# A gated mix of two spectral filters on one core: one product instruction a unit, the negations on VectorE, half of the gate later, and a new order list

## The chip, the cores and the metric

The kernel runs on one core of a Trainium2 chip. The metric is the device time of one execution in microseconds (us); three executions took 115.3, 115.53 and 116.19, median 115.53. TensorE (PE) multiplies matrices into PSUM, VectorE (DVE), ScalarE (ACT) and GpSimd (POOL) do elementwise work, and SyncE (SP) issues nearly all transfers. Each engine works through its own instructions in order.

## The reference

Both branches filter the same `x` (2048 rows by 1024 columns, bf16) in the frequency domain, with weights A and B. A gate per row mixes the two results.

```python
def _ref(x, w_r, w_i):                       # A and B alike
    B, S, D = x.shape
    X = jnp.fft.rfft2(x.astype(jnp.float32), axes=(-2, -1))
    X = X * (w_r + 1j * w_i)
    return jnp.fft.irfft2(X, s=(S, D), axes=(-2, -1)).astype(jnp.bfloat16)

g = sigmoid((x * gate_w).sum(-1, keepdims=True))
return g * _ref(x, A_w_r, A_w_i) + (1 - g) * _ref(x, B_w_r, B_w_i)
```

## The kernel before

The transforms are matrix products with constant matrices. The 2048 rows are taken as 128 x 16 (`s1` from 0 to 15 is a slab of 128 rows), the columns are folded into sums and differences ("even" and "odd" frequencies), and the frequency rows are worked in 16 units: units 0 to 7 are even, 8 to 15 odd. A unit covers two groups of 64 frequency rows, 256 columns each.

The program is written down as a list, `ORDER`. Its tokens are executed from left to right, each calls one small function, and every engine's instructions come in the order of their tokens. So the list alone decides what stands behind what on each engine and in SP's queue of transfers; the tile pools and the semaphores add the waits. A token's last letter often names the engine (A for ScalarE, D for VectorE, P for GpSimd, S for SP), and the last digit of a TensorE token is its PSUM bank (of eight; some take two banks, from that digit on).

The tokens, by stage:

- **Load.** `x:S:s:n` loads n slabs, `c:S:..` constants, `W:S:n` the weights of unit n (512 KB). W 0 to 7 go into the tile `ro`, 8 to 11 into `wx`, 12 to 15 into the tile `y` (once the even half of `y` has been used up). `tab:A` runs a small sigmoid so that ScalarE's function table is loaded.
- **First transform.** `F1:s:e/o` multiplies a slab's half (eight matmuls, L331). Then either `FC` copies one part out of PSUM and `FD` (VectorE, two instructions) folds it into `y`, or `FX` copies both parts and `FP` (GpSimd, two instructions) folds. The copies go to eight rotating pieces of `wx`.
- **Gate.** `GH`, `GC`, `GT` (four times), `GK` compute and turn the gate's transform; `GZ:h` spreads eight slabs of it over the rows (TensorE), `GS:h` takes the sigmoid of these (ScalarE, 1024 columns) into the tile `EA`. `GA:D:b` multiplies four slabs of `EA` by the constant `E`, and `GB:D:b` makes `EB` as `E` less that. `EA` and `EB` are the matrices of the second inverse transform, in which the mixing is done; slabs 8 to 15 are needed by its tokens with v of 4 and above.
- **Unit n.** `F2:n:tt` (four matmuls) and its copy `T`; `F3:n` (twelve matmuls, of which four use `WN`, the negative of the constant `WF`, made by `neg`) and its copy `X`; `P:n:r`, the products of `X` with the weights of both filters (VectorE, L505); for units 0 to 7 a correction of one column, `Y` (TensorE), `NA` and `N` (VectorE); `J:n` (32 matmuls in four groups, L548), into two pairs of banks; two copies `R:n:0` and `R:n:1` into a tile `rl`; two stores `H:n:0` and `H:n:1` (256 KB each) to scratch memory in DRAM.
- **Inverse over rows and columns.** `L:p:v` loads 512 KB of scratch back (p is 0 for the even half, into `re`, 1 for the odd half, into `ro`; v from 0 to 7). `V:p:v:s` (eight matmuls, L576) and its copy `VC`; then `C` (four matmuls of 256 columns, L601) or `U` (four of 512, L592).
- **Output.** For the even half `EX` copies out of PSUM and `EQ` mixes (VectorE or GpSimd, L626), or `ES` and `EF`, or `E`. For the odd half `OR` adds straight from PSUM (VectorE, L646), or `OC` and `OP`, or `QD` and `QP`, use GpSimd. `S:v` stores 512 KB of output, `S:v:s` half of that.

The pools have two buffers each for `T`, `X` and `V`, three for the products `p`, and five for `rl`, which the output tiles share. An `rl` buffer is free when its two stores have landed. On every copy token `cp` (L199 to L203) picks the instruction, so copies of ScalarE have line L201 and those of VectorE L203.

Products may be asked for in halves or at once:

```python
def prod(n, r):                              # L493 to L505
    ...
    if r == "b":
        xb = X[:].rearrange("p r t (a m) -> p r t a m", a=1).to_broadcast([P, 2, 2, 4, 256])
        wb = w.rearrange("p (r t) a m -> p r t a m", r=1).to_broadcast([P, 2, 2, 4, 256])
        nc.vector.tensor_tensor(p[:], xb, wb, ALU.mult)
        return
    xb = X[:, int(r)].rearrange("p t (a m) -> p t a m", a=1).to_broadcast([P, 2, 4, 256])
    nc.vector.tensor_tensor(p[:, int(r)], xb, w, ALU.mult)
```

In the list before, each unit has two tokens, `P:n:0` and `P:n:1`, and on TensorE the order within `J:n` is: first real by real, second imaginary by imaginary (which needs the other half), then the two mixed ones.

The functions that the change calls differently:

Of the kernel before, what the change touches and what calls it, by code (L numbers as in the profile page):

```python
# [10 lines left out]
P = 128  # L11
S = 2048
D = 1024
# [8 lines left out]


ORDER = """
warm:8 c:A:F1 x:S:0:1 x:S:1:1 c:A:gws x:S:2:2 tab:A F1:0:e:4 x:S:4:2 FC:0:e:D F1:1:e:7 F1:0:o:5 x:S:6:2 FC:1:e:A FD:0:e
FX:0:o:A F1:1:o:0 FD:1:e F1:2:e:6 x:S:8:2 FC:2:e:D FX:1:o:A F1:3:e:2 FD:2:e FC:3:e:A FD:3:e FP:1:o FP:0:o x:S:10:2 x:S:12:2
F1:2:o:4 F1:3:o:7 F1:4:e:0 F1:5:e:6 x:S:14:2 FX:2:o:A FP:2:o FC:4:e:D c:S:w0 c:S:WF:0:4 c:S:PM c:S:WF:4:16 c:S:EZ c:S:FD:0:1
W:S:0 W:S:1 c:S:E c:S:WJ:0:4 c:S:WJ:4:16 F1:7:e:1 FC:5:e:A W:S:2 FX:3:o:A FD:4:e FD:5:e FP:3:o F1:6:e:3 FC:7:e:A F1:5:o:4
F1:9:e:0 F1:8:e:6 F1:7:o:5 FC:6:e:A FX:5:o:A FC:9:e:A FD:7:e FD:6:e FC:8:e:A F1:11:e:1 gc:P F1:10:e:7 FX:7:o:A F1:4:o:4
F1:12:e:3 F1:13:e:2 FC:11:e:A FC:10:e:A FP:5:o FD:9:e FD:8:e FD:11:e FX:4:o:A F1:9:o:1 F1:15:e:6 F1:14:e:0 F1:11:o:5 FP:7:o  # L30
FC:12:e:A FC:13:e:A neg:A:0:4 FC:15:e:A FD:10:e FP:4:o FD:12:e FC:9:o:A F1:13:o:7 FC:14:e:A FD:13:e F1:12:o:4 F1:6:o:2
FD:15:e FD:14:e FD:9:o F2:1:0:6 FC:11:o:A neg:A:4:16 FC:13:o:A FX:6:o:A F2:1:1:3 T:1:0:A FD:13:o FC:12:o:A F1:15:o:2 T:1:1:A
FC:15:o:A FD:11:o F1:14:o:1 F1:10:o:0 F3:1:6 F2:0:0:3 F1:8:o:5 FD:12:o FC:10:o:A F2:0:1:4 FC:14:o:A FD:15:o FD:10:o F2:2:0:2
FD:14:o X:1:A FC:8:o:A T:0:0:A pw:P T:0:1:A T:2:0:A FD:8:o F2:3:0:0 F2:2:1:7 T:2:1:A F3:0:5 X:0:A P:1:1 P:1:0 P:0:1 F2:3:1:4
Y:1:3 F2:4:0:7 T:3:1:A FP:6:o F3:2:1 NA:1:D Y:0:5 W:S:9 NA:0:D W:S:3 W:S:7 P:0:0 W:S:8 W:S:11 N:1:D W:S:6 W:S:4 c:S:FD:1:2
W:S:5 c:S:IG T:4:0:A GH:6 X:2:A T:3:0:A GC:A Y:2:4 NA:2:D F2:5:1:1 P:2:0 P:2:1 W:S:10 F3:3:2 T:5:1:A F2:4:1:4 N:0:D GT:2:5
J:1:6:0 GT:0:5 X:3:A GT:1:5 GT:3:5 T:4:1:A F3:4:3 R:1:0:A F2:5:0:2 R:1:1:D X:4:A T:5:0:A GK:D J:0:6:0 F2:6:0:4 P:3:1 F2:6:1:5
Y:3:3 R:0:0:A F3:5:6 R:0:1:A P:3:0 NA:3:D GZ:0:2 F2:7:0:0 X:5:A F2:7:1:1 W:S:14 T:6:1:D T:6:0:D N:3:D N:2:D GS:0 P:4:0
T:7:0:D J:3:4:6 W:S:12 W:S:13 W:S:15 T:7:1:A GZ:1:0 R:3:1:A R:3:0:D J:2:6:2 Y:5:4 P:4:1 GS:1 Y:4:5 NA:5:D NA:4:D P:5:0 P:5:1
R:2:0:A N:4:D F3:7:0 R:2:1:A X:7:A F2:8:1:5 F3:6:6 F2:8:0:4 T:8:0:A T:8:1:D J:4:2:0 F3:8:4 H:0:0 H:1:0 X:6:A R:4:1:A Y:7:7  # L40
P:7:1 F2:9:0:6 N:5:D R:4:0:A Y:6:0 P:7:0 H:1:1 X:8:A NA:6:D T:9:0:A H:0:1 NA:7:D GA:D:4 F2:10:1:1 H:2:0 H:3:0 H:3:1 F2:9:1:0
P:6:0 T:9:1:A N:7:D P:6:1 T:10:1:A J:5:2:4 J:7:0:6 R:5:1:A R:5:0:A F2:10:0:5 H:4:0 F3:9:2 F2:11:0:4 P:8:1 H:2:1 R:7:0:A N:6:D
R:7:1:D J:6:0:6 GB:D:4 H:4:1 T:10:0:A X:9:A H:7:0 H:5:0 P:8:0 T:11:0:D R:6:0:A GA:D:0 R:6:1:A F2:11:1:2 F3:10:3 P:9:0 H:5:1
P:9:1 H:7:1 H:6:1 X:10:A H:6:0 J:8:0:6 T:11:1:A R:8:0:D R:8:1:A F2:12:0:4 H:8:0 T:12:0:A P:10:1 P:10:0 F3:11:2 F2:12:1:5
H:8:1 L:0:0 F2:14:1:1 X:11:A T:12:1:A L:0:1 GB:D:0 F2:14:0:0 F3:12:6 J:9:2:4 T:14:0:A P:11:0 T:14:1:A X:12:A R:9:1:A P:11:1
# [12 lines left out]
VC:1:1:1:A EQ:6:0:1:P EQ:7:0:0:P C:1:3:1:1 QD:3:1:1 V:1:0:0:0 EF:5:0 QD:3:0:0 U:1:1:0:6 U:1:1:1:2 QD:3:1:0 OR:1:1:0 OR:1:1:1
EQ:7:1:1:P EQ:7:0:1:P VC:1:0:1:A EQ:6:0:0:P VC:1:0:0:A OC:1:0:A V:1:2:0:4 QP:3:1:0:P OP:1:0:0 VC:1:2:0:A V:1:2:1:5 V:1:5:0:7
U:1:0:1:6 VC:1:2:1:D OR:0:1:1 U:1:2:0:2 OR:2:0:0 OR:0:1:0 OR:2:0:1 U:1:0:0:0 V:1:5:1:5 QP:3:1:1:P OC:0:0:A VC:1:5:1:A  # L60
QP:3:0:1:P OP:1:0:1 QP:3:0:0:P VC:1:5:0:D S:S:1 U:1:2:1:3 OR:2:1:0 OP:0:0:1 V:1:4:0:0 V:1:4:1:5 OR:2:1:1 S:S:3 VC:1:4:1:D
OP:0:0:0 VC:1:4:0:A U:1:5:0:6 U:1:5:1:4 U:1:4:0:7 V:1:7:1:5 U:1:4:1:1 OC:4:0:A OR:5:0:0 OR:5:1:0 S:S:2 V:1:6:1:7 VC:1:7:1:A
EQ:6:1:0:P OR:5:0:1 OR:5:1:1 OR:4:1:1 OR:4:1:0 U:1:7:1:3 S:S:0 S:S:5 OP:4:0:1 VC:1:6:1:A V:1:6:0:2 OP:4:0:0 VC:1:6:0:A S:S:4
U:1:6:1:6 V:1:7:0:4 U:1:6:0:0 VC:1:7:0:A OR:7:1:1 OR:7:1:0 OR:6:1:0 U:1:7:0:4 OR:6:1:1 OR:6:0:1 OR:6:0:0 OR:7:0:1 OR:7:0:0
S:S:7:1 S:S:6 S:S:7:0
"""


# [655 lines left out]
```

## Time and profile before

| | |
|---|---|
| median of three executions | 115.53 us |
| profiled execution: its own time | 116.1 us |
| its span, first to last instruction | 114.3 us |
| busy: TensorE, VectorE, ScalarE, GpSimd | 103.0, 100.9, 86.4, 39.5 us |
| moved by DMA | 36.79 MB, mean 322 GB/s |
| granted TensorE clock | 0.991 |

The span lies inside the execution's own time; 1.8 us are around it. A line of groups reads: source line, engine, operation, output and input tiles, shape, how many; then busy us, mean ns of one; then the idle time before them and what ended it. A line of a timeline or of the chain begins with start and duration in us. TensorE's matmuls overlap, so a busy TensorE is not one at its peak.

### The profile page before, as it was taken

Reading aid. Unit: us, or ns where it says so; the run is one execution under the profiler, and the core shown is the slowest. Engines: PE = TensorE matmul, PEld = TensorE weight load, DVE = VectorE, ACT = ScalarE, POOL = GpSimd, SP = SyncE. Lnnn points to the kernel's source line nnn. Section 1 sums busy time; section 2 is a strip of 40 time slices with the busy share of each in tenths; the row PEclk is TensorE's granted clock in tenths of the full one; section 3 lists DMA queues with packets and bytes.
Section 4 is the critical chain, followed back from the end, with each engine's and each line's share of the span. In section 5 each row is a group of like instructions: output and inputs, shape, how many; then the busy total and the mean of one; then the engine's idle time right before and its main releaser. Section 6 shows DMA issues by size and latency. Waiting matters only on the chain.

```text
span 114.3 us, 3946 instructions
## 1 busy us (share of the span) xinstructions
PE 103.0 (90%) x1616; PEld 70.3 (61%) x1619; DVE 100.9 (88%) x175; ACT 86.4 (76%) x140; POOL 39.5 (35%) x61
## 2 busy tenths in 40 slices
PE   5969999999999988989898989998999999999930
PEld 2569999875546543534453547845998966566510
DVE  0068999999998999999999999999999598998990
ACT  4054989999799899999999999999689762325400
POOL 1019999800000000000000000830382999997300
PEclk9999999999999999999999999999999999999996
DMA  3999999999999899997969999996999998099655
GB/s 75 330 331 406 405 374 318 350 338 376 398 406 416 257 361 281 376 377 245 339 232 262 393 391 301 369 386 228 335 281 351 377 390 345 3 377 398 271 222 199
DMA packets 17794, 36.79 MB, mean 322 GB/s; under 512 B 1904, under 2 KB 10736, under 8 KB 17776
## 3 DMA queue, kind: packets, MB, share of 16 engines
q1 hardware_dynamic: 17488, 36.44, 88.4%
q8 instruction: 12, 0.20, 0.6%
q10 hardware_dynamic: 288, 0.10, 0.6%
q14 instruction: 6, 0.05, 0.1%
HBM read 23.96 MB, written 12.58 MB: 320 GB/s over the span
## 4 chain that ended last, share of the span: by engine, by line
PE 18%; DMA 10%; ACT 9%; DVE 6%; issue 3%; SPq 3%; DVEq 1%; ACTq 0%
PE ps L592 7%; DMA ro<-sc 7%; PE ps L576 5%; ACT rl L201 4%; DVE p L505 3%; PE ps L548 3%; DMA sc<-rl 3%; DVE ot L646 3%; SPq L565 3%; ACT T L201 2%; ACT X L201 1%; PE ps L485 1%; PE ps L455 1%; ACT V L201 1%; PE ps L601 1%
## 5 line engine op out<-in xcount | busy, mean ns | idle before, releaser
L626 POOL TENSOR_TENSOR re<-wx 128x256 f32<-128x256 f32 x15 | 12.9, 883 | 58.7 <-ACT wx L201 50.0
L201 ACT COPY wx<-ps 128x256 f32<-128x256 f32 (+1 forms) x41 | 18.0, 467 | 12.3 <-PE ps L592 5.7
L201 ACT CAST rl<-ps 128x1024 bf16<-128x1024 f32 x25 | 24.6, 1042 | 0.7 <-PE ps L548 0.7
L548 PE MATMUL ps<-p,wj 32*64 32x512 bf16 x512 | 19.6, 380 | 2.6 <-ACT rl L201 1.4
L505 DVE TENSOR_TENSOR p<-X,ro 128x2048 bf16<-128x2048 bf16 x16 | 19.1, 1218 | 0.0
L455 PE MATMUL ps<-fd,y 128*128 128x256 bf16 x128 | 17.7, 273 | 0.4 <-ACT rl L201 0.2
L201 ACT CAST V<-ps 128x512 bf16<-128x512 f32 x23 | 13.0, 593 | 6.3 <-PE ps L576 4.8
L201 ACT CAST X<-ps 128x1024 bf16<-128x1024 f32 x16 | 16.7, 1044 | 0.2 <-PE ps L485 0.2
L331 PE MATMUL ps<-f,re 128*128 128x128 bf16 x256 | 15.9, 225 | 0.9 <-DMA re<-in_x_dram 0.9
L331 PEld LDWEIGHTS <-re 128*128 128x128 bf16 x256 | 15.4, 101 | 1.9 <-DMA re<-in_x_dram 1.4
L379 DVE TENSOR_TENSOR y<-ps,wx 128x256 bf16<-128x256 f32 x48 | 16.3, 416 | 0.1
L201 ACT CAST T<-ps 128x512 bf16<-128x512 f32 x26 | 15.2, 628 | 0.8 <-PE ps L485 0.8
L646 DVE TENSOR_TENSOR ot<-re,ps 128x512 bf16<-128x512 f32 x22 | 13.9, 683 | 0.9 <-PE ps L592 0.5
L548 PEld LDWEIGHTS <-wj 32*64 32x64 bf16 x512 | 8.2, 103 | 10.4 <-issue 6.8
L455 PEld LDWEIGHTS <-y 128*128 128x128 bf16 x128 | 11.1, 97 | 5.0 <-issue 3.8
L379 POOL TENSOR_TENSOR y<-wx 128x256 bf16<-128x256 f32 x16 | 11.1, 731 | 7.3 <-ACT wx L201 7.3
L592 PE MATMUL ps<-ig,V 128*128 128x512 bf16 x53 | 13.2, 379 | 0.2
L485 PE MATMUL ps<-T,wf 64*64 64x512 bf16 (+1 forms) x128 | 10.4, 334 | 0.6 <-ACT T L201 0.3
L505 DVE TENSOR_TENSOR p<-X,y 128x2048 bf16<-128x2048 bf16 x8 | 9.9, 1282 | 0.0
L601 PE MATMUL ps<-ig,V 128*128 128x256 bf16 x72 | 9.8, 273 | 0.0
L505 DVE TENSOR_TENSOR p<-X,wx 128x2048 bf16<-128x2048 bf16 x8 | 9.5, 1218 | 0.0
L203 DVE COPY wx<-ps 128x256 f32<-128x256 f32 (+1 forms) x8 | 4.2, 549 | 5.9 <-PE ps L331 5.9
(61 smaller groups left out, 144.3 us busy)
## 6 DMA issues: line engine op xcount, KB each, us to landing
sc<-rl SPq DMA_DIRECT2D x32, 256.0 KB, 5.5
ro<-in_we_dram SPq DMA_DIRECT2D x8, 512.0 KB, 6.9
re<-sc SPq DMA_DIRECT2D x8, 512.0 KB, 7.1
ro<-sc SPq DMA_DIRECT2D x8, 512.0 KB, 6.3
re<-in_x_dram SPq DMA_DIRECT2D x7, 512.0 KB, 9.0
out_dram<-ot SPq DMA_DIRECT2D x7, 512.0 KB, 2.7
wx<-in_wo_dram SPq DMA_DIRECT2D x4, 512.0 KB, 7.2
y<-in_wo_dram SPq DMA_DIRECT2D x4, 512.0 KB, 6.6
```

Source lines behind the costliest of these rows:

```text
L201: nc.scalar.copy(out=out, in_=in_)
L331: nc.tensor.matmul(o, lhsT=lh, rhs=rh, start=(h == 0), stop=(h == 1))
L379: Q[e].tensor_tensor(yo[:, v, k:k + n, s1, :], a.rearrange("p (k c) -> p k c", c=4), b.rearrange("p (k c) -> p k c", c=4), op)
L455: nc.tensor.matmul(ps[:, v * 256:v * 256 + 256], lhsT=y[:, v, par, b, 2 * t:2 * t + 2, :, :].rearrange("p j s c -> p (j s c)"), rhs=C["FD" ...
L485: nc.tensor.matmul(view(ps[ho, tt * 512:(tt + 1) * 512], dst), lhsT=lh, rhs=view(T[hp(jh), tt, :], src), start=(w == 0), stop=(w == 1))
L505: nc.vector.tensor_tensor(p[:, int(r)], xb, w, ALU.mult)
L548: nc.tensor.matmul(o, lhsT=lh, rhs=src[r, ri, wi, tt], start=(q == 0), stop=(q == 3))
L576: nc.tensor.matmul(ps[:, ch * 128:ch * 128 + 128], lhsT=RR[par][:, v, ch // 2, s, c0 + 256 * ab:c0 + 256 * ab + 128], rhs=Ew[:, s1, :], st ...
L592: nc.tensor.matmul(ps, lhsT=Vs[par, v][:, s, ch, :], rhs=rh, start=(ch == 0), stop=(ch == 3))
L601: nc.tensor.matmul(ps[:, o:o + 256], lhsT=Vs[par, v][:, s, ch, :], rhs=g[:, o:o + 256], start=(ch % 2 == 0), stop=(ch % 2 == 1))
L626: Q[e].tensor_tensor(EV[:, v, s, 256 * h:256 * h + 256], t[:, 0], t[:, 1], (ALU.add, ALU.subtract)[h])
L646: nc.vector.tensor_tensor(otile(v)[:, s, h, :], EV[:, v, s], PS["O", 1, v, s], (ALU.add, ALU.subtract)[h])
```

## The change

Only `ORDER` is changed (591 tokens before, 575 after). All functions, tiles, pools and constants stay. What the new list does, counted token by token:

- Every unit has one token `P:n:b` in place of `P:n:0` and `P:n:1`: one VectorE instruction of 4096 elements a partition in place of two of 2048.
- `neg:A:0:4` and `neg:A:4:16` become `neg:D:0:4` and `neg:D:4:16`.
- `GZ:1`, `GS:1` and what follows from them for slabs 8 to 15 move: before, `GZ:1` and `GS:1` stand between `J:3` and `J:2`; now `GZ:1:3` stands behind `J:12` (banks 3 and 4) and `GS:1` behind `R:12:1`.
- Some copies change between ScalarE and VectorE. VectorE now has two `FX` (0 before), two `FC` (3), five `R` (7), seven `T` (6), one `X` (0), six `VC` (9), six `EX` (4), two `ES` (1), one `E` (0).
- `tab:A` stands behind the first ScalarE copy, `FC:1:e:A`; the built program has two loads of ScalarE's function table, one ahead of each of the two.
- Units, banks, stores and loads come in another order: the stores of units 1 to 4 ahead of `W:S:12` and `W:S:15`; `H:11` ahead of the second half of `H:9`; the odd loads as 3, 1, 0, 2, 5, 6, 4, 7; the last output stores are `S:4`, `S:7:1`, `S:6` (before: `S:7:1`, `S:6`, `S:7:0`).

The diff, cut to the lines that these points and the prediction speak of:

```diff
 ORDER = """
-warm:8 c:A:F1 x:S:0:1 x:S:1:1 c:A:gws x:S:2:2 tab:A F1:0:e:4 x:S:4:2 FC:0:e:D F1:1:e:7 F1:0:o:5 x:S:6:2 FC:1:e:A FD:0:e
-FX:0:o:A F1:1:o:0 FD:1:e F1:2:e:6 x:S:8:2 FC:2:e:D FX:1:o:A F1:3:e:2 FD:2:e FC:3:e:A FD:3:e FP:1:o FP:0:o x:S:10:2 x:S:12:2
...
-FC:12:e:A FC:13:e:A neg:A:0:4 FC:15:e:A FD:10:e FP:4:o FD:12:e FC:9:o:A F1:13:o:7 FC:14:e:A FD:13:e F1:12:o:4 F1:6:o:2
...
-W:S:5 c:S:IG T:4:0:A GH:6 X:2:A T:3:0:A GC:A Y:2:4 NA:2:D F2:5:1:1 P:2:0 P:2:1 W:S:10 F3:3:2 T:5:1:A F2:4:1:4 N:0:D GT:2:5
-J:1:6:0 GT:0:5 X:3:A GT:1:5 GT:3:5 T:4:1:A F3:4:3 R:1:0:A F2:5:0:2 R:1:1:D X:4:A T:5:0:A GK:D J:0:6:0 F2:6:0:4 P:3:1 F2:6:1:5
-Y:3:3 R:0:0:A F3:5:6 R:0:1:A P:3:0 NA:3:D GZ:0:2 F2:7:0:0 X:5:A F2:7:1:1 W:S:14 T:6:1:D T:6:0:D N:3:D N:2:D GS:0 P:4:0
-T:7:0:D J:3:4:6 W:S:12 W:S:13 W:S:15 T:7:1:A GZ:1:0 R:3:1:A R:3:0:D J:2:6:2 Y:5:4 P:4:1 GS:1 Y:4:5 NA:5:D NA:4:D P:5:0 P:5:1
...
-U:1:6:1:6 V:1:7:0:4 U:1:6:0:0 VC:1:7:0:A OR:7:1:1 OR:7:1:0 OR:6:1:0 U:1:7:0:4 OR:6:1:1 OR:6:0:1 OR:6:0:0 OR:7:0:1 OR:7:0:0
-S:S:7:1 S:S:6 S:S:7:0
+warm:8 c:A:F1 x:S:0:1 x:S:1:1 F1:0:o:4 F1:0:e:0 F1:1:o:5 c:A:gws F1:1:e:1 x:S:2:2 F1:3:e:6 FC:1:e:A tab:A FC:0:e:D FX:0:o:D
+FX:1:o:A x:S:4:2 F1:2:e:3 x:S:6:2 x:S:8:2 F1:3:o:7 x:S:10:2 x:S:12:2 F1:2:o:5 FD:0:e c:S:E x:S:14:2 FD:1:e FC:3:e:D FP:0:o
+FC:2:e:A FD:3:e FD:2:e F1:5:e:1 FX:2:o:A FC:5:e:A F1:4:e:4 F1:5:o:3 c:S:EZ c:S:w0 c:S:FD:0:1 F1:6:e:0 FC:4:e:A FX:3:o:D
...
+W:S:7 W:S:0 T:0:1:A FD:12:o FC:10:o:A T:0:0:A F1:9:o:1 FC:9:o:A W:S:3 neg:D:0:4 FD:14:o F3:1:2 neg:D:4:16 FD:10:o FD:15:o
...
+P:1:b T:3:1:A T:2:0:A F2:5:0:1 W:S:4 NA:1:D NA:0:D FD:8:o P:0:b N:1:D F2:4:0:0 F3:2:2 F3:3:4 FP:6:o T:5:0:A c:S:WJ:0:4 W:S:10
+W:S:6 T:4:0:A c:S:WJ:4:16 W:S:8 W:S:9 X:2:A T:4:1:D P:2:b W:S:5 X:3:A N:0:D GH:6 J:1:2:0 Y:2:4 Y:3:7 c:S:IG GC:A W:S:11
+NA:2:D GT:3:5 GT:1:5 R:1:0:A GT:2:5 GT:0:5 F2:5:1:6 GK:D R:1:1:A F3:4:2 T:5:1:A J:0:4:0 NA:3:D F3:5:6 X:4:A P:3:b F2:7:1:2
...
+R:3:1:A Y:5:2 F3:7:0 T:6:1:D NA:5:D GA:D:4 N:4:D W:S:13 J:2:6:2 W:S:14 H:1:1 R:3:0:A X:7:D R:2:1:A R:2:0:A H:1:0 H:0:1 H:3:1
...
+T:13:0:D F3:14:2 X:14:A P:12:b J:11:0:6 V:0:0:0:5 R:11:1:A F3:13:2 VC:0:0:0:A R:11:0:A X:13:A J:12:4:6 F2:15:0:1 P:14:b
+V:0:1:1:0 F2:15:1:2 T:15:0:D L:0:3 T:15:1:D VC:0:1:1:D V:0:0:1:1 R:12:0:A GZ:1:3 C:0:0:0:5 R:12:1:A GS:1 VC:0:0:1:A C:0:1:1:0
+V:0:1:0:7 F3:15:2 P:13:b C:0:0:1:1 EX:1:1:A X:15:A EX:0:1:A L:0:2 EX:0:0:D GA:D:8 V:0:2:1:0 L:0:4 VC:0:1:0:D V:0:2:0:6
+J:13:4:2 VC:0:2:1:A L:0:7 H:9:0 H:11:0 VC:0:2:0:A H:11:1 H:9:1 H:10:0 H:12:1 J:14:0:6 P:15:b R:14:1:D R:13:1:A R:13:0:A
+H:12:0 J:15:4:2 H:10:1 R:14:0:A GA:D:12 GB:D:8 EQ:1:1:1:P H:13:1 H:13:0 C:0:2:0:7 GB:D:12 EX:2:0:D C:0:1:0:0 R:15:0:A
+V:0:4:1:6 EX:1:0:D V:0:4:0:5 R:15:1:A V:0:6:1:7 VC:0:4:0:A C:0:2:1:3 VC:0:4:1:D EX:2:1:A C:0:4:0:2 V:0:6:0:4 EQ:1:0:1:D
...
+OR:7:1:0 U:1:6:0:6 S:S:7:0 OR:6:1:0 OR:6:1:1 OR:6:0:1 OR:6:0:0 S:S:4 S:S:7:1 S:S:6
 """
```

## The prediction

> **What bounds the kernel now.** I read the page first, then the busy time by stage, the groups by shape, the timeline around the last products, and the chain that ended last.
>
> The page's first part says that no engine is free: TensorE (PE), VectorE (DVE) and ScalarE (ACT) are all busy for most of the span. An average cannot say which one sets the end.
>
> ```profile
> PE 103.0 (90%) x1616; PEld 70.3 (61%) x1619; DVE 100.9 (88%) x175; ACT 86.4 (76%) x140; POOL 39.5 (35%) x61
> ```
>
> So I cut the span where the work changes kind: 9.0 (from here VectorE runs almost without a break), 36.1 (TensorE stops being gapless), 78.9 (last inverse product J:15 done), 109.6 (last matmul).
>
> ```profile
> core 0: us, PE busy (x) PEld busy (x) DVE busy (x) ACT busy (x) POOL busy (x), PEclk, DMA share, GB/s
> 0.00:9.00 9.00, 6.89 (x52) 4.47 (x53) 2.21 (x7) 2.94 (x5) 1.15 (x7) 1.00 0.79 250
> 9.00:36.10 27.10, 26.82 (x507) 21.12 (x505) 26.57 (x61) 24.04 (x49) 13.17 (x30) 1.00 1.01 378
> 36.10:78.90 42.80, 38.86 (x743) 22.01 (x742) 42.23 (x55) 42.09 (x57) 3.25 (x2) 1.00 0.95 326
> 78.90:109.60 30.70, 30.45 (x321) 22.70 (x324) 28.19 (x52) 17.34 (x32) 21.95 (x23) 1.00 0.83 309
> 109.60:114.30 4.70, 0.04 (x1) 0.00 (x0) 1.70 (x3) 0.00 (x0) 0.00 (x0) 0.78 0.44 176
> ```
>
> In the second row TensorE (26.8 of 27.1) and VectorE (26.6) are both full. In the third, VectorE (42.2 of 42.8) and ScalarE (42.1) are full and TensorE has gaps. In the fourth TensorE is full (30.45 of 30.7). So VectorE and ScalarE together decide when J:15 ends, and from there 30.7 us of gapless TensorE work and 4.7 us of ending follow. The clock column is 1.00 throughout the work, so it plays no part.
>
> The prices are in the groups by shape (busy us, mean ns) and in one line of VectorE's timeline.
>
> ```profile
> L201 ACT CAST rl<-ps 128x1024 bf16<-128x1024 f32 x25 | 24.6, 1042 | 0.7 <-PE ps L548 0.7
> ...
> L505 DVE TENSOR_TENSOR p<-X,ro 128x2048 bf16<-128x2048 bf16 x16 | 19.1, 1218 | 0.0
> ...
> L203 DVE CAST rl<-ps 128x1024 bf16<-128x1024 f32 x7 | 8.5, 1221 | 0.3
> ...
> L431 ACT ACTIVATE ea<-ps 128x1024 bf16<-128x1024 f32 x2 | 2.1, 1042 | 0.0
> ...
> L442 DVE TENSOR_TENSOR ea<-ea,e 128x512 bf16<-128x512 bf16 x4 | 1.7, 416 | 0.0
> ...
> L278 ACT ACTIVATE wn<-wf 128x768 bf16<-128x768 bf16 x1 | 0.9, 857 | 0.0
> ```
> ```profile
> 24.50 3.49 DVE L505 TENSOR_TENSOR p<-X,ro 128x2048 bf16<-128x2048 bf16 x3
> ```
>
> Three products take 3.49 us, so a second one costs (3.49-1.22)/2 = 1.135: an instruction overlaps its neighbour by 0.085. Below, VectorE's prices are means less 0.085, ScalarE's means less 0.1.
>
> Two more pieces of the timeline: the start of ScalarE, and the last products beside GpSimd (POOL).
>
> ```profile
> 1.62 1.28 ACT L296 ACT_TABLE_LOAD   x1 [1.62 <-PEq L704]
> 2.91 0.21 ACT L296 ACTIVATE junk<-junk 128x8 f32<-128x8 f32 x1
> ```
> ```profile
> 70.67 4.02 DVE L505 TENSOR_TENSOR p<-X,y 128x2048 bf16<-128x2048 bf16 x3
> ...
> 72.02 3.25 POOL L626 TENSOR_TENSOR re<-wx 128x256 f32<-128x256 f32 x2 [49.69 <-ACT wx L201]
> ```
>
> Three products cost 4.02 here against 3.49 above: 0.53 is lost while GpSimd mixes even rows (1.6 us each; the group mean of these is 0.88). The chain's last third shows the handover to the end:
>
> ```profile
> 78.75 1.93 ACT rl L201 x2
> ...
> 81.04 3.23 DMA sc<-rl
> ...
> 87.68 7.81 DMA ro<-sc
> ...
> 107.56 2.54 DVE ot L646 x4
> ```
>
> J:15's two copies (R:15), their stores, the loads of the odd half, TensorE, four adds, a store.
>
> **The change part by part.**
>
> *One product a unit.* Sixteen instructions of 4096 elements for 32 of 2048. Rows of 512 (416 ns) and 2048 (1218 ns) of bf16 pairs give 0.522 ns an element and 0.15 fixed; 4096 costs 2.29, or 2.20 in a train. 16 x 2.20 - 32 x 1.135 = -1.1 us. The other end: the wider pattern loses the fast rate and runs at that of the 1024-element f32 copy (1221 ns, 1.04 ns an element): 4.4 us each, +33 us. Both operands still run along one step with only repeats above, as in the row, so I take -1.1. No matmul starts later by it: J's second group of matmuls needs both halves already, and for units 0 to 7 the patch N stands behind both.
>
> *Moves between VectorE and ScalarE.* Counted up to the last product P:15, VectorE gains FX:0 and FX:3 (2 x 0.60), X:7 (1.14), one T (0.60), one EX (0.60), GA:8 (0.33), and loses two R (2 x 1.14) and one FC (0.33): +1.3. FX:0 falls in the time before 9.0 where VectorE waits for x, so +0.7 counts. The negations have no row on VectorE. At the bf16 pair rate (L442) they cost 0.2 + 0.47; at one element a cycle (L203) 0.33 + 0.87; at best the fixed part, 0.15. I take 0.5. "VectorE: DVE Perf Modes" of the Trainium skill (section "The perf-mode tier table") gives single-source bf16 work four elements a cycle; by it they would be an estimated 0.22 + 0.36 before overlap, 0.1 us below my value. No run here shows it yet. Sum for VectorE up to P:15: -1.1 + 0.7 + 0.5 = +0.1 us on 66.4 us of work. Measured, this took 68.6 (9.0 to 77.6): 2.1 went to waits and to the 0.53.
>
> ScalarE up to R:15:1 loses two FX (0.98), one T (0.52), X:7 (0.94), EX (0.50), the negations (1.08), and gains two R (1.88) and one FC (0.28): -1.9 us.
>
> *Where the waits go.* GK now follows P:2 directly, with no R copy between; the four GT turns come after J:1 on TensorE, which is gapless there, so GK waits about 0.6, and P:3 behind it. The waits of before at 35.8 and 39.5 (0.4 and 0.1) and around the Y patches go. EX:0:0 on VectorE sets GpSimd's mixes beside P:15, so I leave the 0.53 in. Stores H:1 to H:4 pass W:12 and W:15 in SP's queue, and so free rl buffers earlier; W:12 and W:15, behind them, are wanted 15 us later. I end P:15 at 77.4, 0.2 earlier.
>
> *The sigmoid's second half.* GZ:1 (eight matmuls) and GS:1 (1.04 on ScalarE) move from 40 us to between R:12 and X:15. GZ:1 writes banks 3 and 4, F3:15 bank 3, so X:15 waits for GS:1. Counting ScalarE on from P:12's end, X:15 ends some 0.3 us before VectorE wants it: hidden, with almost no cover. GA:12, GB:8 and GB:12 then stand ahead of V:0:4, where TensorE still has two C groups and reaches it later.
>
> *Stores and buffers.* R:13's buffer is now freed by the third store after the loads L:0 (H:11), no longer by one long done; at 0.67 us for 256 KB (390 GB/s, as in the page's fuller slices) it comes within 0.4 us of the copy. Bounds: 0 to 1.3; I take 0.1. So J:15 ends 0.1 earlier in all.
>
> *The end.* V:1:3 comes one C group (0.44) sooner in TensorE's list while its load keeps its distance from R:15, and loads already hold TensorE for 0.3: +0.3. The last store is S:6, 512 KB (median 2.7 to landing), no longer 256 KB (2.4); by the two last stores themselves 2.6 against 2.1: +0.4. The adds behind the last U stay four.
>
> *The start.* tab:A now stands behind FC:1, and ScalarE loads tables twice, the second time at about 7.8 to 9.1. FX:1 and FC:2 follow; FC:2 ends at 10.1, FD:2 wants it at 10.2. Cost 0, cover 0.1.
>
> **The sum.** -0.1 + 0.3 + 0.4 = +0.6. The profiled execution took 116.1 (span 114.3, 1.8 around it), so its like would take 116.7. The median of the runs is 115.53, 0.6 below that execution; on its scale I predict **116.1**.
>
> **The rivals.**
>
> *Faster: the freed time shows.* For it: ScalarE has 1.9 us less before R:15, and both engines are full in the third row. If VectorE's 2.1 us of waits halve and the 0.53 goes, J:15 ends 1.6 earlier: 115.5 - 1.6 + 0.5 = 114.4, and 113.9 if the end costs nothing. Against it: VectorE's work is the same, and each of its 20 copies can wait for TensorE. 0.22.
>
> *Slower: the late sigmoid.* The place is GS:1 before X:15. If ScalarE is over 0.3 us behind there, each further us goes straight to P:15 and J:15. Price up to GS:1 + GZ:1 = 1.04 + 0.45, less the 0.3: 116.1 + 1.2 = 117.3. For it: ScalarE is full from 42 to 81. 0.16.
>
> *Slower: the second table load.* FC:2 has 0.1 us of cover. If the switch costs twice the load's row, VectorE starts its train 1.2 us later, and 0.6 may be absorbed in the GK wait: 116.7 to 117.3. Against it: in the trace the next ScalarE instruction starts 0.01 us after the load, though nothing ran ahead of it. "ScalarE: Activation LUTs" of the Trainium skill (section "What ACT_TABLE_LOAD costs") speaks for this rival: it adds 1380 ns of draining to a load of 1283 ns. The trace has the same 1283; the draining no run here shows. 0.12.
>
> *Slower: the wide product loses its rate*: 116 + 33 = 149. 0.02. *R:13 waits its full 1.3 for a store*: 117.3. 0.05.
>
> **How the numbers follow.** Forecast 0.43; rivals as above. About 1% (1.15 us) is what a measurement of this kernel tells from no change. Faster (under 114.4): 0.18 of the first rival and 0.06 of the forecast's own spread, 0.24. Slower (over 116.7): 0.11 + 0.08 + 0.02 + 0.04 of the rivals and 0.09 of the forecast's, 0.34. Same: 0.42. The forecast's own range is 115.0 to 117.0; the full one, 114.0 to 118.3, reaches past the first rival and past two of the slower ones together.
>
> **What would show it.** Products of 2.2 to 2.3 us; negations of 0.2 to 0.5 on VectorE; a table load near 7.8 us with FC:2 ending by 10.2; GK idle 0.6; P:15 ending near 77.4 and R:15:1 near 80.5; first odd V waiting for its load; TensorE ending near 110. Wrong if VectorE idles over 1 us ahead of P:15, or J:15 ends outside 77.5 to 80.

## The result, and the profile after

The changed kernel takes 1.0057 of the time of the kernel before, 95% interval 1.0029 to 1.0084: half a per cent slower, within the 1% that the prediction called no change, though the interval leaves out 1. The medians of all 18 executions are 117.0 and 115.95 us; the ratio leaves out the slower of two states in which executions come (5 of these 18 of the changed kernel), so the medians don't divide into it. The profiled execution took 117.08 us with a span of 115.3, against 116.1 and 114.3.

In the changed file every helper stands one line higher: the copies are L200 (ScalarE) and L202 (VectorE), `F3` is L484, `J` is L547, and the merged product is L501, inside the branch `r == "b"`. First the line of busy times, to be read beside the first one of the prediction: VectorE has 163 instructions, no longer 175, and its busy time is 100.6, no longer 100.9.

```profile
PE 101.1 (88%) x1616; PEld 71.2 (62%) x1619; DVE 100.6 (87%) x163; ACT 85.9 (74%) x137; POOL 40.2 (35%) x61
```

The same stages as before (stretch, its length, then busy time and instructions of each engine, granted clock, DMA share, GB/s):

```profile
core 0: us, PE busy (x) PEld busy (x) DVE busy (x) ACT busy (x) POOL busy (x), PEclk, DMA share, GB/s
...
9.00:36.10 27.10, 25.48 (x500) 20.66 (x500) 27.00 (x60) 22.89 (x48) 12.67 (x29) 1.00 1.02 383
36.10:78.90 42.80, 37.56 (x734) 23.19 (x731) 41.87 (x44) 41.48 (x55) 4.68 (x3) 1.00 0.93 321
78.90:109.60 30.70, 30.11 (x334) 22.50 (x322) 26.23 (x50) 18.09 (x33) 21.17 (x22) 1.00 0.79 293
```

VectorE is fuller than before from 9.0 to 36.1 (27.00 of 27.10) and TensorE emptier (25.48, before 26.82). From 78.9 TensorE lacks 0.3 us that it had before (30.11 against 30.45). The clock is 1.00 in these three stretches.

The added 1.0 us of span splits by three points of the two traces. J:15's last matmul ends at 79.22 (before 78.88): +0.34. TensorE ends at 110.41 (before 109.64), 31.19 after J:15 and no longer 30.76: +0.43 (0.29 of it is the wait for the first odd load, shown below; in the kernel before no wait of TensorE over 0.15 stands there). From there to the span's end it is 4.90, no longer 4.68: +0.22.

**The handover.** The chain that ended last shows the first of these (start, duration, what):

```profile
77.08 1.03 ACT rl L200
78.11 0.04 issue
78.15 1.08 PE ps L547 x32
...
84.15 4.76 DMA ro<-sc
88.91 0.05 issue
88.96 1.07 PE ps L575 x16
```

J:15 begins at 78.15, directly behind ScalarE's copy R:13:0, although the last product P:15 had ended at 77.43. Further down, the first odd V begins when its load has landed, at 88.91. ScalarE's timeline says why the copy was late (in brackets: idle time, and what ended it):

```profile
74.67 1.09 ACT L200 CAST V<-ps 128x512 bf16<-128x512 f32 x2
76.17 2.84 ACT L200 CAST rl<-ps 128x1024 bf16<-128x1024 f32 x3 [0.41 <-DMA sc<-rl]
```

The three copies are R:13:1, R:13:0 and R:14:0. The first waited 0.41 for a store out of the `rl` buffer that it reuses. By these rows J:15 could have begun up to 0.4 earlier without that wait; n2 below takes it away.

**The negation.** VectorE, GpSimd and TensorE at 21 to 23 us, three views:

```profile
20.82 1.36 DVE L279 TENSOR_SCALAR wn<-wf 128x256 bf16<-128x256 bf16 x1
22.10 0.74 DVE L378 TENSOR_TENSOR y<-ps,wx 128x256 bf16<-128x256 f32 x2
22.77 0.34 DVE L279 TENSOR_SCALAR wn<-wf 128x768 bf16<-128x768 bf16 x1
```
```profile
20.66 1.44 POOL L378 TENSOR_TENSOR y<-wx 128x256 bf16<-128x256 f32 x2
```
```profile
22.99 0.41 PE L484 MATMUL ps<-T,wf 64*64 64x512 bf16 x4 [1.12 <-DVE y L378]
```

The negation of 256 elements takes 1.36 us, that of 768 elements 0.34. The short one lies beside GpSimd's last fold FP:6 (20.66 to 22.10) and ends 0.08 after it. Behind it waits the fold FD:14:o, which reads PSUM bank 2, and bank 2 is the one that F3:1 is to write: TensorE idles 1.12. This was not in the prediction; n4 and q2 below try the cause.

**The start and the merged product.**

```profile
6.83 0.37 ACT L200 COPY wx<-ps 128x256 f32<-128x256 f32 x1 [3.93 <-PE ps L330]
7.22 1.28 ACT L295 ACT_TABLE_LOAD   x1
...
8.63 0.84 ACT L200 COPY wx<-ps 128x512 f32<-128x512 f32 x2
```
```profile
75.15 2.28 DVE L501 TENSOR_TENSOR p<-X,y 128x4096 bf16<-128x4096 bf16 x1
```
```profile
74.38 3.63 POOL L625 TENSOR_TENSOR re<-wx 128x256 f32<-128x256 f32 x2
```

The second table load lies at 7.22 to 8.50; FC:2 (second of the two copies) ends at 9.47 and FD:2 begins at 9.50. The last product took 2.28 us (all sixteen lie between 2.27 and 2.29), though GpSimd mixed beside it; here it was GpSimd that gave way: its second instruction (EQ:0:0:0) began at 75.18, just behind the product, and ended at 78.01, 2.84 us for an operation that takes 0.73 when VectorE runs no product.

### The profile page after: what moved, and what is told of

The parts are those of the page before. It is cut to its first block, busy times and chain, and to the rows that moved or that the text cites. A ratio compares the mean times of both kernels' runs of the same rounds, so it can differ in the third digit from the quotient of the medians.

```text
span 115.3 us, 3931 instructions
## 1 busy us (share of the span) xinstructions
PE 101.1 (88%) x1616; PEld 71.2 (62%) x1619; DVE 100.6 (87%) x163; ACT 85.9 (74%) x137; POOL 40.2 (35%) x61
## 4 chain that ended last, share of the span: by engine, by line
PE 35%; DMA 26%; DVE 15%; ACT 12%; issue 5%; SPq 3%; DVEq 1%; ACTq 0%
DMA re<-sc 10%; DVE y L378 10%; PE ps L591 8%; DMA sc<-rl 7%; PE ps L547 7%; ACT rl L200 6%; PE ps L575 6%; DMA wx<-in_wo_dram 4%; DMA ro<-sc 4%; DVE ot L645 3%; PE ps L244 3%; ACT X L200 3%; PE ps L484 3%; SPq L564 2%; PE ps L454 2%
## 5 line engine op out<-in xcount | busy, mean ns | idle before, releaser
L200 ACT CAST rl<-ps 128x1024 bf16<-128x1024 f32 x27 | 26.7, 1054 | 1.4 <-PE ps L547 1.0
L200 ACT CAST V<-ps 128x512 bf16<-128x512 f32 x26 | 14.7, 595 | 9.8 <-PE ps L575 5.5
L200 ACT COPY wx<-ps 128x256 f32<-128x256 f32 (+1 forms) x37 | 15.4, 456 | 8.1 <-PE ps L330 5.4
L547 PE MATMUL ps<-p,wj 32*64 32x512 bf16 x512 | 18.5, 380 | 2.7 <-ACT rl L200 1.7
L501 DVE TENSOR_TENSOR p<-X,ro 128x4096 bf16<-128x4096 bf16 x8 | 18.2, 2278 | 0.0
L200 ACT CAST X<-ps 128x1024 bf16<-128x1024 f32 x15 | 15.7, 1065 | 1.4 <-PE ps L484 1.2
L200 ACT CAST T<-ps 128x512 bf16<-128x512 f32 x25 | 14.4, 636 | 0.8 <-ACT T L200 0.8
L547 PEld LDWEIGHTS <-wj 32*64 32x64 bf16 x512 | 8.6, 103 | 9.6 <-issue 5.9
L484 PE MATMUL ps<-T,wf 64*64 64x512 bf16 (+1 forms) x128 | 9.9, 332 | 3.2 <-DVE y L378 1.1
L202 DVE COPY wx<-ps 128x512 f32<-128x512 f32 (+1 forms) x12 | 7.0, 596 | 6.5 <-PE ps L330 4.8
L484 PEld LDWEIGHTS <-wf 64*64 64x64 bf16 x128 | 4.7, 105 | 7.4 <-issue 5.5
L501 DVE TENSOR_TENSOR p<-X,wx 128x4096 bf16<-128x4096 bf16 x4 | 9.1, 2282 | 0.0
```

Source lines behind the costliest of these rows:

```text
L200: nc.scalar.copy(out=out, in_=in_)
L202: Q[e].tensor_copy(out=out, in_=in_)
L484: nc.tensor.matmul(view(ps[ho, tt * 512:(tt + 1) * 512], dst), lhsT=lh, rhs=view(T[hp(jh), tt, :], src), start=(w == 0), stop=(w == 1))
L547: nc.tensor.matmul(o, lhsT=lh, rhs=src[r, ri, wi, tt], start=(q == 0), stop=(q == 3))
```

## The experiments

The kernels m1 to m4 ran on one chip, n1 to n4 on another, q1 to q4 on a third. Ratios are to the kernel before, run beside them on the same chip; profile rows come from one execution each. Only the third chip also ran the changed kernel itself (q1), so on the other two a variant's distance from the changed kernel is known less finely. Executions differ from each other at the very start already: VectorE's first fold begins at 6.45 us in one execution of the changed list and its variants and at 7.45 in another, so a row is compared by what lies between it and its neighbours.

**m1: the kernel before with merged products, nothing else.** The first of each unit's two tokens is left out and the second becomes `P:n:b`, for example:

```diff
-... F2:11:0:4 P:8:1 H:2:1 R:7:0:A N:6:D
-R:7:1:D J:6:0:6 GB:D:4 H:4:1 T:10:0:A X:9:A H:7:0 H:5:0 P:8:0 T:11:0:D ...
+... F2:11:0:4 H:2:1 R:7:0:A N:6:D
+R:7:1:D J:6:0:6 GB:D:4 H:4:1 T:10:0:A X:9:A H:7:0 H:5:0 P:8:b T:11:0:D ...
```

> The kernel before, with one product instruction a unit and nothing else changed. In the changed kernel a merged product took 2.28 us and the next began 0.08 before its end, so merging saves 2 x 1.135 - 2.20 = 0.07 a unit, 1.1 us on VectorE in all. Theory (two engines share the bound): ScalarE is as full as VectorE from 42 to 81 us, so only part of the 1.1 shows: P:15 ends 0.3 to 1.1 earlier than 77.6 us, R:15:1 at most 0.3 earlier than 80.7, ratio to the kernel before 0.997 (0.994 to 1.000). Rival A (VectorE alone sets the end of J:15): the whole 1.1 shows, ratio 0.990. Rival B (the longer instruction holds back the short copies and patches behind it): ratio 1.004 or more.

Measured: 1.0161 [1.011, 1.0212]. The theory's 0.997 is missed, and the ratio lies where rival B put it. The saving on VectorE's busy time is there (100.0 us, no longer 100.9), and the kernel is slower. VectorE's timeline around unit 8, in this kernel and then in the kernel before:

```profile
51.22 0.23 DVE L530 TENSOR_TENSOR p<-np 128x16 bf16<-128x16 f32 x1
52.30 1.22 DVE L202 CAST rl<-ps 128x1024 bf16<-128x1024 f32 x1 [0.86 <-PE ps L547]
```
```profile
50.55 1.22 DVE L505 TENSOR_TENSOR p<-X,wx 128x2048 bf16<-128x2048 bf16 x1
51.69 0.22 DVE L531 TENSOR_TENSOR p<-np 128x16 bf16<-128x16 f32 x1
51.77 1.22 DVE L203 CAST rl<-ps 128x1024 bf16<-128x1024 f32 x1
```

In the kernel before, the half product P:8:1 at 50.55 fills the time in which R:7:1 would have to wait for TensorE. Merged, it is gone from there, and R:7:1 idles 0.86. The same happens at NA:0 (0.75), NA:2 (0.53), R:3:0 (0.70) and, behind a copy of ScalarE's, at R:12:1 (0.91). From 9.0 to the end of P:15 VectorE idles 4.50 us here and 1.06 in the kernel before; P:15 ends at 79.47, no longer 77.56. So the merge can pay only together with an order that has other work for those places. The changed list has it: 1.03 us of idle time in the same stretch. That the longer instruction itself holds others back (rival B) is not ruled out: TensorE idles 1.06 ahead of J:13 and 0.87 ahead of J:15 for a merged product here. And the merged product always stands at the place of the second token; the place of the first was not tried.

**m2 and q4: the changed kernel with two products a unit again** (the same kernel on two chips).

```diff
-... X:4:A P:3:b F2:7:1:2
+... X:4:A P:3:1 P:3:0 F2:7:1:2
```

> The changed kernel with each product split into its two halves again. Theory: VectorE pays 1.1 us more by P:15. In the changed kernel J:15 waited for R:13:0 until 78.10 us and not for P:15, which ended at 77.43, so 0.7 of the 1.1 is hidden there unless R:13 moves too: total 0.4 to 1.1 us more than the changed kernel, ratio to the kernel before 1.009 to 1.015 (the changed kernel has 1.006). Rival (the merge bought nothing, ScalarE or the stores set the pace): 1.006.

> The changed kernel with two products a unit again, second time, now beside the changed kernel itself. Theory (16 merged instructions save 1.1 us of VectorE's time, and VectorE has almost no waits that would hide them): ratio to the kernel before 0.004 to 0.009 above the control's. Rival (J:15 waits for R:13's copies on ScalarE, so VectorE's time is hidden there): within 0.003 of the control's.

Measured: m2 1.0153 [1.0094, 1.0211]; q4 1.0118 [1.0045, 1.0191], beside a control (q1, below) of 1.0073. By the midpoints the merge is worth 0.45% in the changed list, in the direction and of the size that the theory asks for, but the intervals of q4 and q1 overlap, so it is not settled. m2 lies just above its theory's range. The profiles don't settle it either: P:15 ends at 77.94 in m2 and 78.17 in q4, 0.5 to 0.7 later than the 77.43 of the changed kernel. In both, the last half product takes 1.75 us and no longer 1.21, beside GpSimd's mixes, so that 0.53 of this difference is the loss that the kernel before has too, and not the fixed cost of a second instruction. J:15 ends at 79.06 and 79.29, within 0.2 of the 79.22 of the changed kernel. In m2 it begins right behind the product, and in q4 too (after 1.29):

```profile
77.99 1.07 PE L547 MATMUL ps<-p,wj 32*64 32x512 bf16 x32 [1.28 <-DVE p L504]
```

R:13:0 had ended shortly before, at 77.83 and 78.03. In the changed kernel the product is done 0.7 earlier, and J:15 waits for R:13:0 until 78.10: in these rows, what the merge wins up to P:15 is lost to that copy. These are rows of the shortest execution of both. Where the others lose their time, no profile shows.

The same kernel gave 1.0153 on one chip and 1.0118 on another: ratios from different chips are not compared more finely than this.

**m3: the negations back on ScalarE.**

```diff
-W:S:3 neg:D:0:4 FD:14:o F3:1:2 neg:D:4:16 FD:10:o
+W:S:3 neg:A:0:4 FD:14:o F3:1:2 neg:A:4:16 FD:10:o
```

> The changed kernel with the two negations on ScalarE again, at the same places of the list. On VectorE they took 1.36 and 0.34 us, 1.5 us of its train. Theory: VectorE is then held by X:1 on ScalarE, which follows the two negations (0.42 and 0.86) there and ends near 24.7, so P:1 starts 0.3 earlier than 25.0 us and not 1.5: 0 to 0.4 us less than the changed kernel, ratio to the kernel before 1.002 to 1.006. Rival A (VectorE's whole 1.5 us comes off): ratio 0.993. Rival B (ScalarE is the bound, so 1.1 us more on it costs as much): 1.012.

Measured: 1.0205 [1.0152, 1.0258], more than the theory and either rival; against m2 on the same chip half a per cent more. On ScalarE the two take 1.22 us (22.50 to 23.72), X:1 follows, and P:1 idles 0.62 for it. P:1 begins 0.36 us earlier than in the changed kernel all the same (24.66 against 25.02), and the lead is gone at GK, which here idles 1.06 (the last 22 of TensorE's 64 small matmuls for the turns begin 1.29 late, for nothing that the profile shows). P:3 ends at 36.84, against 35.81. So by the total, even at 1.36 + 0.34 us the negations are no worse on VectorE in this list; how much of the 0.9 us of span between m3 (116.2) and the changed kernel is ScalarE's load and how much that wait, this one execution can't say.

**m4: the sigmoid's second half early again**, between J:3 and T:6.

```diff
-... J:3:4:6 T:6:0:A
+... J:3:4:6 GZ:1:0 T:6:0:A GS:1
...
-... R:12:0:A GZ:1:3 C:0:0:0:5 R:12:1:A GS:1 VC:0:0:1:A
+... R:12:0:A C:0:0:0:5 R:12:1:A VC:0:0:1:A
```

> The changed kernel with GZ:1 (banks 0 and 1) and GS:1 back behind J:3, at about 40 us. Theory: where it stands in the changed kernel the sigmoid is hidden (X:15 ended at 74.29 us and P:15 began only at 75.15), and early it delays F3:7, which needs banks 0 and 1, and with it X:7 on VectorE by 0.6 us: 0 to 0.6 us more than the changed kernel, ratio to the kernel before 1.006 to 1.011. Rival (the late sigmoid holds J:15 through R:12, X:15 and R:13 on ScalarE): J:15 ends up to 1.0 us earlier than 79.2, ratio 0.997.

Measured: 1.0222 [1.0161, 1.0282], far above the theory's 1.011. The rival falls. Early, GZ:1 stands in banks 0 and 1 (bank 0 is also its place in the kernel before), which F3:7 writes next; TensorE waits 1.05 us for GS:1 (40.32 to 41.34) to empty them, and VectorE's copy X:7 waits for F3:7:

```profile
42.14 1.22 DVE L202 CAST X<-ps 128x1024 bf16<-128x1024 f32 x1 [1.04 <-PE ps L484]
```

P:5 behind it ends at 45.56, not 44.10, and the 1.4 us are still there at P:15 (78.85 against 77.43). So the price is that of this place, its banks included; another early place was not tried. Late, it holds no product up: in the changed kernel X:15 ends at 74.29 and P:15 begins at 75.15, a cover of 0.9 us.

**n1: the table load ahead of ScalarE's copies**, as the only one.

```diff
-... c:A:gws F1:1:e:1 x:S:2:2 F1:3:e:6 FC:1:e:A tab:A FC:0:e:D
+... c:A:gws tab:A F1:1:e:1 x:S:2:2 F1:3:e:6 FC:1:e:A FC:0:e:D
```

> The changed kernel with tab:A ahead of FC:1 again, so that ScalarE loads its function table once. In the changed kernel the second load ran from 7.22 to 8.50 us, FC:2 ended at 9.47 and FD:2 began at 9.50, 0.10 after VectorE was free. Theory (hidden): at most 0.1 us less, ratio to the kernel before 1.005 to 1.006. Rival (the load delays the start): 1.2 us less, ratio 0.995.

Measured: 1.0056 [1.0011, 1.0101], the changed kernel's own ratio. The second load is hidden.

**n2: R:13's buffer freed earlier**, by another order of the four stores of units 9 and 11.

```diff
-H:9:0 H:11:0 VC:0:2:0:A H:11:1 H:9:1 H:10:0
+H:9:0 H:9:1 VC:0:2:0:A H:11:0 H:11:1 H:10:0
```

> The changed kernel with both stores of unit 9 ahead of those of unit 11. R:13 takes the rl buffer whose stores were written down first. In the changed kernel that is H:11, the third store behind the loads (landed 76.08 us), and R:13:1 began at 76.17 after 0.41 of idle ScalarE; J:15 waited for R:13:0 until 78.10. Theory (the store is the wait): the buffer is free at the second store, 0.7 earlier, R:13:1 starts near 75.8, J:15 ends 0.4 earlier, the total is 0.3 to 0.5 less, ratio to the kernel before 1.002. Rival (R:13 waited for J:13 or the copies ahead of it): nothing changes, 1.006.

Measured: 1.008 [1.003, 1.0129]: no gain. The wait itself is gone; ScalarE's copies follow the V copies directly:

```profile
75.03 1.09 ACT L200 CAST V<-ps 128x512 bf16<-128x512 f32 x2
76.04 2.84 ACT L200 CAST rl<-ps 128x1024 bf16<-128x1024 f32 x3
```

From the end of the V copies to the end of J:15 it is 2.97 us (76.12 to 79.09), against 3.46 in the changed kernel (75.76 to 79.22) and 3.71 in n1, whose wait was 0.66. So the place is right, and in these rows half a microsecond is won there, but this execution was later from its first folds on, and no total shows the gain. The expected ratio was missed.

**n3: the last output store in two halves.**

```diff
-... S:S:4 S:S:7:1 S:S:6
+... S:S:4 S:S:7:1 S:S:6:1 S:S:6:0
```

> The changed kernel with the last output store, 512 KB, written as two of 256 KB; the first of them needs only the first two of the last four adds. The last store of the changed kernel landed 2.61 us after its issue, the last of the kernel before (256 KB) 2.09. Theory: the end comes 0.3 to 0.5 us earlier, ratio to the kernel before 1.002. Rival (landing depends on what else is under way, or SP's extra issue of 0.35 us eats it): 1.006.

Measured: 0.9999 [0.9947, 1.005], against 1.0056 and 1.008 of the two kernels beside it that end as the changed kernel does; the three intervals overlap. From TensorE's last matmul to the end of the span it is 4.22 us, no longer 4.90. The traces are surer than the totals here: in the ten of the changed kernel and its variants that end on 512 KB this stretch is 4.88 to 4.90, and in q3 below, whose last store is split as well, it is 4.22 again. This is the largest single part of the loss that an experiment shows, and this kernel has the lowest ratio of the family: as fast as the kernel before as far as its interval tells, and not shown to be faster.

**n4: the negation measured by itself.** Four more copies of the short negation (256 elements, into a part of `EB` that is free at that time) at places where GpSimd is at work or idle.

```diff
-FD:15:e FD:14:e FD:11:o ...  FD:13:o FC:12:o:A ...  FD:9:o X:1:A
+FD:15:e np:D FD:14:e FD:11:o ...  FD:13:o np:D FC:12:o:A ...  np:D FD:9:o np:D X:1:A
```

> The changed kernel with four more copies of the small negation (256 elements a partition, into a free part of EB) on VectorE: behind FD:15:e and FD:13:o, when GpSimd is at work on FP:4, pw and FP:6, and two after 24 us, when GpSimd has nothing to do. Theory (VectorE waits until GpSimd is between instructions or done): the two early ones take 0.5 us or more, ending as a run of GpSimd instructions ends, the two late ones 0.2 to 0.3. Rival A (the first negation pays a start of its own): only the first is long. Rival B (the constant's transfer, or the strided reading of WF): all four are as long as 1.36. The total time says nothing here: VectorE has up to 3 us of work more.

Measured, VectorE and then GpSimd (the copies are L283, the original is L279):

```profile
18.37 0.83 DVE L283 TENSOR_SCALAR eb<-wf 128x256 bf16<-128x256 bf16 x1
...
21.12 0.53 DVE L283 TENSOR_SCALAR eb<-wf 128x256 bf16<-128x256 bf16 x1
...
22.24 0.21 DVE L279 TENSOR_SCALAR wn<-wf 128x256 bf16<-128x256 bf16 x1
```
```profile
20.84 1.42 POOL L382 TENSOR_TENSOR y<-wx 128x256 bf16<-128x256 f32 x2
```

The same instruction takes 0.83 and 0.53 us beside GpSimd's folds, and 0.21 behind the last of them, at 22.24; the two later copies (24.63 and 25.43) take 0.21 each as well. The original, which took 1.36 in the changed kernel, is one of the fast ones here only because the copies pushed it to 22.24, where the last fold ends. In n1, where the negation happened to begin 0.04 us into the last fold and had that one alone to sit through, it took 0.78. That GpSimd's work is the cause is shown. "VectorE: DVE Perf Modes" of the Trainium skill (section "The perf-mode tier table") gave an estimated 0.22 and 0.36 for the two negations; with GpSimd idle the trace has 0.21 and 0.34 and agrees. "SBUF — State Buffer" (section "SBUF: two separate sides") says that VectorE, in a two-port mode or with two SBUF inputs against a GpSimd instruction that reads SBUF, shares a pair of ports with GpSimd as an exclusive lock: whoever starts first keeps it for the whole instruction. The rows agree as to the blocking: the delayed negation ends 0.08 after a fold of GpSimd's, and EQ:0:0:0, which began 0.03 after the last product, ended 0.58 after that product's end.

**q1: the changed kernel again, as a control on the third chip.**

> The changed kernel as it is, the control for the three beside it on the same chip. Theory: 1.006 of the kernel before, as measured at first. Rival (chips differ for this list more than the interval says): 1.012 or more, as the four variants that were run on another chip without this control.

Measured: 1.0073 [1.0037, 1.011], the first result again within its interval. In the profiled executions of q1 and q2 the granted clock falls to 0.50 in the middle of the work (q1 from 79.6 to 83.0 us, q2 from 35.0 to 38.4), so rows behind these times are not read.

**q2: the short negation behind two more folds.**

```diff
-W:S:3 neg:D:0:4 FD:14:o F3:1:2 neg:D:4:16 FD:10:o FD:15:o
+W:S:3 FD:14:o FD:10:o neg:D:0:4 F3:1:2 neg:D:4:16 FD:15:o
```

> The changed kernel with the first negation behind two more folds (FD:14:o, FD:10:o), ahead of F3:1 still; it then begins when GpSimd has done its last fold FP:6. Theory (the negation took 1.36 us because GpSimd was at work, and it held back the fold whose bank F3:1 wants): it takes 0.2 us, TensorE's idle time before F3:1 falls from 1.1 to under 0.6, P:1 begins 0.6 to 1.0 us earlier. How much of that is left at the end: by the prediction's own step GK would then wait about 0.6 for TensorE's turns, and J:15 waits for R:13's copies anyway, so the span changes by no more than -0.2 us, ratio to the kernel before within 0.003 of the control. Rival (VectorE is the bound up to P:15): P:15 ends 0.6 to 1.0 earlier and the ratio falls by 0.005 or more.

Measured: 1.0067 [1.0029, 1.0106], 0.0006 below the control, so the theory's "within 0.003" holds by the midpoints and the rival's 0.005 is not seen, with intervals of 0.004 to either side. The negation takes 0.22, TensorE's idle time before F3:1 falls from 1.07 in the control to 0.42, and P:1 begins at 24.02 against the control's 24.66 (the clock is 1.00 in this stretch in both). Then GK waits 1.21 for TensorE's turns and the lead is lost: P:3 begins at 33.96, the control's at 33.26. The turns are 64 small matmuls, and here as in m3 they stop behind the 42nd:

```profile
33.39 0.30 PE L417 MATMUL ps<-one,eb 1*32 1x1 bf16 x22 [1.53 <-issue]
```

The clock is still 1.00 then, and the profile shows no cause; in the control the same gap is 0.50, in the changed kernel 0.18. Without the gap the turns would by these rows have been done near 32.2, and VectorE came to GK at 32.56, so this is no proof of the wait that the theory names. q3, which has the same edit, answers it. That the 0.6 us don't show in the total is what the ratio says.

**q3: three edits together**, q2's, n3's and an earlier R:13:1.

```diff
-VC:0:2:1:A L:0:7 H:9:0 H:11:0 VC:0:2:0:A H:11:1 H:9:1 ... P:15:b R:14:1:D R:13:1:A R:13:0:A
+VC:0:2:1:A H:9:0 H:11:0 H:11:1 L:0:7 R:13:1:A VC:0:2:0:A H:9:1 ... P:15:b R:14:1:D R:13:0:A
```

> q2_neg_behind_folds, and two more edits: the last output store in two halves, and R:13:1 ahead of the copy VC:0:2:0 with the stores of units 9 and 11 ahead of the load L:0:7. Theory: the last store gives 0.5 us (as measured alone), and with R:13's copies 0.6 us earlier J:15 follows P:15 directly and its end comes 0.4 to 0.7 us earlier, the rest of the program being gapless TensorE work: span 1.0 to 1.3 us under the control's, ratio 0.995 to 0.998 of the kernel before. Rival (J:15's wait only turns into a wait for the odd loads, as at V:1:3): only the 0.5 of the last store shows, ratio about 1.001.

Measured: 1.0053 [1.0013, 1.0093], only 0.002 below the control, and neither 0.995 to 0.998 nor the rival's 1.001. The last store's part is there again (4.22 us from TensorE's end to the span's), though the total is closer to the control than n3 was to its neighbours. The cheap negation's part is there too, and it passes GK:

```profile
32.86 0.30 PE L417 MATMUL ps<-one,eb 1*32 1x1 bf16 x22 [0.16 <-issue]
```
```profile
33.33 0.16 DVE L202 CAST zt<-ps 128x16 bf16<-128x16 f32 x1
```

GK (at 33.33) follows VectorE's work without a wait. n2's profiled execution has its first fold at the same 7.45 and the negation of 1.31: against it q3's P:1 begins 0.91 us earlier (24.86), its P:3 0.77 earlier (33.51), its P:15 ends 0.60 earlier (77.19), and its J:15 ends only 0.11 earlier. So most of the negation's time comes through to P:15, and it is ahead of J:15, at ScalarE's copies, that it is lost; how much of that is due to q3's third edit, these two executions don't separate. The edit of R:13 moved the wait instead of taking it away:

```profile
75.44 1.01 ACT L200 CAST rl<-ps 128x1024 bf16<-128x1024 f32 x1 [0.41 <-PE ps L547]
76.35 0.59 ACT L200 CAST V<-ps 128x512 bf16<-128x512 f32 x1
```
```profile
77.00 1.99 PE L547 MATMUL ps<-p,wj 32*64 32x512 bf16 x60 [1.42 <-ACT V L200]
```

R:13:1 is 0.73 earlier, but the copy VC:0:2:0 behind it is 1.2 later, and J:14 writes the bank that this copy empties. TensorE idles 1.42 inside J:14, where it idled 1.28 ahead of J:15; J:15 ends at 78.98, 0.24 earlier, and right behind it TensorE idles 0.45 for VectorE's copy R:14:1, which is later too (78.15, no longer 77.35). At this place ScalarE has three copies of 1.0 us and one of 0.6 in a row, and TensorE's last two inverse products want all of them.

## Why the prediction was right, and where it was not

The forecast was +0.6 us, under the 1% that was called no change; the profiled execution took 1.0 longer, and the ratio of 1.0057 on 115.95 is 0.66 us. The total is right, in part by luck: some of its steps are right only in their sum.

- **Merged products.** 2.28 us each (predicted 2.29); in the train P:10, P:11 the second starts 2.20 behind the first. The price is right, the rival of the lost rate is out; that the 1.1 us show in the total is not settled (m2 and q4). What the prediction did not say is that the merge needs the new order: alone it loses 1.6% (m1).
- **The negations.** This term of the sum was mis-sized: 0.5 taken, within bounds of 0.15 to 1.2, and 1.36 + 0.34 = 1.70 less overlap measured. The bounds went by the price of the instruction alone; the row of before that showed the contention (three products in 4.02 instead of 3.49 beside GpSimd) was read for the products and not applied to the negation.
- **GK's wait** of 0.6 is not there: the turns were done at 33.04, and VectorE came to GK at 33.36. It isn't there with a cheap negation either (q3: 33.16 and 33.33), as TensorE goes on earlier too (it idles 0.43 ahead of F3:1 there, 1.12 in the changed kernel). Where GK did wait, in m3 and q2, a gap in TensorE's turns without a known cause made it.
- **The waits of before** were over-counted: the sum took 2.1 us for them and the 0.53, but the trace of before has only 1.06 of idle time on VectorE from 9.0 to the end of P:15, 1.6 with the 0.53. So the faster rival, priced at half of those waits, had less to win than it was given.
- **The 0.53 beside GpSimd** that I left in is gone: the merged P:15 came first, and GpSimd waited. These three errors, +1.0 for the negation, -0.6 for GK and -0.5 here, cancel by luck, and P:15 ended at 77.43 against a forecast of 77.4.
- **R:13's wait for a store** was also mis-sized: 0.1 taken with bounds 0 to 1.3; 0.41 in the changed kernel, 0.66 in n1 and 0.53 in n3. With it J:15 ended 0.34 later than before, not 0.1 earlier, and R:15:1 at 81.18, not near 80.5. This is the step that failed with an effect on the end: the wait for the store, and not P:15, set the start of J:15.
- **The first odd V** idles 0.29 for its load, as predicted (0.3). The size is in part luck: the prediction lets loads hold TensorE for 0.3 in the kernel before already, where the trace has no wait over 0.15, and in the variants this wait runs from 0.15 at most (n2, n3, q3) to 0.38 (n1). TensorE's end at 110.41 is near the forecast of 110.
- **The last store.** From the end of the last add to the end of the span it is 3.54 against 3.02, +0.5 as the two kinds of store had said (0.4). Net of it, the adds themselves end 1.36 after TensorE, no longer 1.66, so only 0.22 of it shows between these two traces; n3 gives 0.68.
- **The late sigmoid** is hidden with 0.9 us, more than the 0.3 that I counted; its rival is out, and m4 shows the opposite case.
- **The second table load** is hidden (n1). The load itself took 1.28 us, which agrees with the 1283 ns of "ScalarE: Activation LUTs" (section "What ACT_TABLE_LOAD costs") of the Trainium skill; the draining of 1380 ns that the page adds is not in the trace: the load began 0.02 us after the copy ahead of it had ended and the next instruction 0.01 after the load, with work ahead of it this time.
- **The faster rival** (the freed time shows at the end) did not happen. In the changed kernel what VectorE and ScalarE gain ends in the wait ahead of J:15, which a copy and a store set.
- **The signs.** Three of those named were not seen: negations of at most 0.5 (1.36), GK's idle 0.6, and R:15:1 near 80.5 (81.18). Of the two that would have made it wrong, J:15 ended at 79.22, within the bounds; VectorE has 1.03 us of idle time over the whole stretch and none right ahead of P:15, so that this one holds or not by how it is read.

What stays open: whether the merge pays in the changed list, where the longer executions of m2 and q4 lose their time, why the first odd load lands later in some executions, and why TensorE's turns stop for 1.3 us in m3 and 1.5 in q2 and for 0.2 in the changed kernel.

## What to carry to other kernels

Before merging two instructions on a full engine, look at what stands between them: a half that fills another engine's delay is worth more than the fixed cost that the merge saves, and the merge can pay only if the new order puts other work there. Price an instruction that moves to VectorE by the rows beside GpSimd's work, not by its element count, and move it to where GpSimd rests. Look at the last transfer first: half its size gave 0.7 us in the trace, more than any edit in the full stretch, where taking away a wait gave the next one. And before a wait is read as the price of an edit, look for a gap in the engine that it waits for: the same wait can be absent in the next execution.

## What the runs showed of the hardware that was not expected

A copy with a factor of 256 bf16 elements on VectorE took 0.21 us with GpSimd idle, and 0.53, 0.78, 0.83 and 1.36 beside GpSimd's folds, each time ending about 0.08 after one of the folds. The profile shows all of it as busy time, none as a wait. In the changed kernel it sat through the rest of one fold instruction and the whole of the next; in n4, from a like start, only through the rest of one. The product of 4096 elements kept its 2.28 when it started first, and a GpSimd mix of 0.73 us then took 2.84. In m1, where a mix had started before it, the product P:13 took 2.82.
